# One unit of look-ahead between two halves of a matmul group, extended to the first block of a fused FFT + MoE kernel

## Chip, cores and metric

The kernel runs as one program on one core of a Trainium2 chip. Its metric is the device time of an execution in microseconds (us); the median of three runs stands for a kernel.

## The reference, cut to what matters

```python
X = np.fft.fft(x, axis=1)             # x: (8, 3072, 256)
X = np.fft.fft(X, axis=2).real        # -> tokens (24576, 256)
h = X @ w_in                          # first MoE layer, d_ff = 2048
g = h * (1.0 / (1.0 + np.exp(-1.702 * h)))
x2 = g @ w_out
logits = x2 @ w_gate                  # 8 experts, one expert for each token, with a capacity
# each kept token: gate * relu(x2 @ w1[e]) @ w2[e], all others stay 0
```

## The kernel before, in words

The FFT over the sequence is a matmul with cosine and sine tables on TensorE (tile `pf`, line 546). Its result goes to DRAM (`uv`). The FFT over the 256 columns is folded into the first layer's weights, which a *conversion* at the start turns into a table `G`, 2048 columns wide.

Then comes phase 2, which makes the routing logits of every token. For each of 8 batches there are 4 *blocks* of some 384 frequencies, and each block has 16 *units* (`f` from 0 to 15), one for each 128 hidden columns. A unit has two halves:

- **E** (`m1_even`, line 755): three matmuls into a PSUM bank `eo`. VectorE then makes a tile `e` from that bank (line 757).
- **O** (`m1_odd`, line 768): three more matmuls, accumulated into the *same* bank. VectorE then makes `h` (tile `h` or `g`, line 770) from `e` and the bank.

O adds to the bank that VectorE's `e` has to read first, so O of a unit can't begin before `e` of that unit is done. After O, ScalarE applies the gelu in place (lines 782 and 783, issued one unit later, in `gelu`), and every fourth unit TensorE multiplies the finished tiles into the block's logits (tile `acc`, line 792). There are 4 `eo` banks, which rotate.

I write E3 or O3 for the halves of unit 3 of the first block, and e3 for its tile `e`. All engines run their own instructions in the order in which the program is written; there is no scheduler. So the order of the lines in `phase2` is the order of each engine's queue.

In the first block of the first batch the conversion is still going on between the units. One weight slice follows another: VectorE and ScalarE convert a slice, TensorE transposes it (`psT`, line 274) or multiplies it by a DFT matrix (`psG`, line 250), ScalarE and VectorE copy the result into a piece of `G` (lines 253 and 254), and small matmuls `psc` (line 262) and `psW` (line 283) make a correction and a part of the router's weights. Batch 0's last FFT matmuls (`pf`) are spread over the units 0 to 4 as well. After unit 10 the conversion's memory is given back, and the loads of the next batch's input (`xc`, line 309) begin in it; line 397 is ScalarE's first use of them. In units 8 to 12 the second block's operand is prepared: transposes `psuv` (line 726), copied to `uvt` by ScalarE and VectorE (lines 731, 732), and a broadcast `psb` (line 741).

Of the kernel before, what the change touches and what calls it, by code (L numbers as in the profile page):

```python
# [23 lines left out]
B, S, D = 8, 3072, 256  # L24
# [10 lines left out]
NFC = DFF // P  # L35
# [8 lines left out]
NU, CONV, OWN, START1, START = 64, 10, 18, 26, 0  # L44
# [16 lines left out]
TICKS, WAIT0 = range(0, 13, 2), (2, 0, 1, 0, 1, 0, 1, 0)  # L61
AGE = (0, 2, 3, 4, 6)
HALVES = 1
HP, GP, LOGITS = 3, 6, 4


# [111 lines left out]
class K:  # L178
# [334 lines left out]
    def merge_half(self, b):  # L513


        x = self.half[b] = self.scp.tile([P, 4 * ZW], F16, tag="half", bufs=HALVES, name="half")
        for l, t in enumerate((self.hi[b, 1], self.lo[b, 1])):
# [508 lines left out]
    def phase2(self):  # L1026
        nc = self.nc
        self.lt, self.info, self.addr = {}, {}, {}
        self.hn = 0
        blocks = [(b, i) for b in range(B) for i in range(4)]  # L1030

        self.parts = [[([(0, 3, 0)], 0, 3)], [([(3, 3, 0)], 3, 3)], [([(6, 3, 0)], 6, 3)],
                      [([(9, 3, 0), (0, 4, 1), (4, 4, 1), (8, 4, 1)], 9, 15)]]
        self.whole = [([(0, 4), (4, 4), (8, 4)], 0, 24)]
        gs, pend, after = {}, [], []
        clears = self.clears()
        hprev, evens = None, []
        accs = {}

        def flush_logits():  # L1040
            j, q, tiles = pend.pop(0)
            b, i = blocks[j]
            if q == 0:
                accs[j] = self.bank("acc", "acc")
            self.m1_logits(b, i, q, tiles, accs[j])
            if q == NFC // 2 - 1:
                after.append((b, i, accs.pop(j)))

        def evac():
            while after:  # L1050
                b, i, acc = after.pop(0)
                self.m1_evac(b, i, acc)

        def gelu(hp):
            j, f, h = hp
            gs.setdefault((j, f // 2), []).append(self.m1_gelu(*blocks[j], f, *h))
            if f % 2 == 1:
                pend.append((j, f // 2, gs.pop((j, f // 2))))

        pre, post = self.timetable()  # L1060

        def take(todo):
            while todo:
                next(todo.pop(0), None)

        for j, (b, i) in enumerate(blocks):
            for f in range(NFC):
                if j == 0:
                    next(self.conv, None)
                evac()  # L1070
                take(pre[NFC * j + f])
                u = NFC * j + f
                while len(evens) < min(1 if u < NFC - 1 else 2, NU * B - u):
                    v = u + len(evens)
                    evens.append(self.m1_even(*blocks[v // NFC], v % NFC))
                self.now = evens[-1][1]
                if hprev is not None:
                    gelu(hprev)
                hprev = (j, f, self.m1_odd(b, i, f, *evens.pop(0)))
                if f % LOGITS == 1:  # L1080
                    while pend:
                        flush_logits()
                if j == 0:
                    next(self.conv, None)
                take(post[NFC * j + f])
                if f == 8 and j >= 4:
                    next(clears, None)
        gelu(hprev)
        while pend:
            flush_logits()  # L1090
        evac()
        self.last_route()
# [348 lines left out]
```

## Time and profile before

| | |
|---|---|
| three runs | 1908.97, 1911.43, 1918.87 us; median 1911.43 |
| profiled execution | 1909.04 us, of which the span from the first to the last instruction is 1907.3 us |
| mean granted TensorE clock | 0.981 of full speed |
| busy share of the span | TensorE 96%, VectorE 61%, ScalarE 50%, GpSimd 32% |

The busy shares are means over the whole execution, and it has stages with different limits; the stage that the change touches lies between 65 and 156 us. The granted clock is 1.0 at 2.4 GHz and 0.5 at 1.2 GHz. In a timeline a bracket gives the engine's idle time just ahead of a row and what ended it.

### The profile page before, as it was taken

To read this page: it belongs to the slowest core of one execution; us is meant where nothing else is said; L and a number is where in the kernel's file an instruction comes from. 1 tells how busy PE (TensorE), PEld (TensorE's weight loads), DVE (VectorE), ACT (ScalarE), POOL (GpSimd) and SP (SyncE) were. 2 spreads that over 40 slices of the span, in tenths; PEclk is the share of its full clock that TensorE was granted. 3 is DMA by queue.
4 is the path that set the end of the run, shared out by engine and by line. 5 is a ranking of instruction groups with operands and counts; after the bars stand their busy time and mean duration, and the time that the engine had idled before them with its cause. 6 is when DMAs were issued, how large, how long until landed. Compare 5 with 4: busy or idle time off the path is not lost.

```text
span 1907.3 us, 34052 instructions
## 1 busy us (share of the span) xinstructions
PE 1824.4 (96%) x12801; PEld 1600.1 (84%) x12801; DVE 1169.6 (61%) x2498; ACT 957.6 (50%) x2133; POOL 608.9 (32%) x776
## 2 busy tenths in 40 slices
PE   3879999999999999999999799999999999999998
PEld 3756778777778787877876599999999999999998
DVE  9636687686867768677689554444444454545442
ACT  5436776676766767766666233333333232333322
POOL 5006437539084481832318511111111100111101
PEclk9778999999999999999999899999999999999999
DMA  8411324232332323222112011111101010101000
GB/s 300 138 59 51 104 66 130 79 108 88 100 100 68 118 80 114 83 67 79 51 55 59 15 56 40 37 42 34 45 24 55 15 50 16 42 28 44 23 9 17
DMA packets 104181, 128.26 MB, mean 67 GB/s; under 512 B 15540, under 2 KB 89636, under 8 KB 103760
## 3 DMA queue, kind: packets, MB, share of 16 engines
q1 hardware_dynamic: 91992, 112.92, 18.6%
q0 software_dynamic: 11008, 12.82, 2.5%
q8 instruction: 100, 1.64, 0.4%
q14 instruction: 65, 0.53, 0.1%
q10 hardware_dynamic: 1016, 0.35, 0.1%
HBM read 77.54 MB, written 47.62 MB: 66 GB/s over the span
## 4 chain that ended last, share of the span: by engine, by line
PE 85%; DVE 8%; issue 4%; ACT 1%; POOL 1%; DMA 1%; POOLq 0%; ACTq 0%; DVEq 0%; SPq 0%
PE pkh L1200 14%; PE py L1214 14%; PE eo L768 13%; PE eo L755 12%; PE acc L792 9%; PE pod L1247 7%; PE pku L1233 7%; PE pf L546 6%; DVE e L757 3%; PE psG L250 1%; PE psuv L726 1%; DVE lo L489 1%; DVE g L770 1%; PE psL L830 1%; PE psb L741 1%
## 5 line engine op out<-in xcount | busy, mean ns | idle before, releaser
L757 DVE SCALAR_TENSOR_TENSOR e<-ub,cf,eo 128x384 f32<-128x384 f32 (+1 forms) x512 | 312.9, 611 | 204.0 <-PE eo L755 186.3
L768 PE MATMUL eo<-uvt,G 128*128 128x384 f32 (+1 forms) x1536 | 365.2, 346 | 31.9 <-DVE e L757 30.5
L755 PE MATMUL eo<-uvt,G 128*128 128x384 f32 (+1 forms) x1536 | 384.2, 358 | 0.3
L768 PEld LDWEIGHTS eo<-uvt,G 128*128 128x128 f32 x1536 | 272.5, 190 | 57.4 <-DVE e L757 56.3
L1200 PE MATMUL pkh<-kx,G 128*128 128x384 f32 x1536 | 310.5, 340 | 0.1
L1214 PE MATMUL py<-kg,wo 128*128 128x384 f32 x1536 | 307.1, 337 | 0.0
L755 PEld LDWEIGHTS eo<-uvt,G 128*128 128x128 f32 x1536 | 258.7, 190 | 40.2 <-issue 36.9
L1214 PEld LDWEIGHTS py<-kg,wo 128*128 128x128 f32 x1536 | 272.1, 187 | 0.0
L1257 POOL DMA_INDIRECT out_dram<-ko,tl x48 | 50.3, 1048 | 690.0 <-ACT ko L1256 680.2
L1200 PEld LDWEIGHTS pkh<-kx,G 128*128 128x128 f32 x1536 | 265.9, 189 | 0.8 <-ACT kx L1190 0.5
L1203 ACT ACTIVATE kgf<-pkh 128x384 f32<-128x384 f32 x256 | 125.8, 492 | 269.0 <-PE pkh L1200 180.7
L782 ACT ACTIVATE g<-g 128x384 f32<-128x384 f32 (+1 forms) x341 | 179.0, 525 | 145.0 <-DVE g L770 134.3
L1204 DVE CAST kg<-kgf 128x384 fp32r<-128x384 f32 x256 | 95.8, 374 | 218.5 <-ACT kgf L1203 217.6
L916 POOL DMA_INDIRECT table<-info,ad x192 | 190.3, 991 | 50.6 <-issue 47.6
L770 DVE SCALAR_TENSOR_TENSOR g<-e,eo 128x384 f32<-128x384 f32 (+1 forms) x341 | 187.3, 549 | 11.1 <-PE eo L768 11.1
L783 ACT ACTIVATE g<-eo 128x384 f32<-128x384 f32 (+1 forms) x341 | 163.8, 480 | 0.2
L1235 ACT ACTIVATE krl<-pku 128x384 fp32r<-128x384 f32 x128 | 62.9, 492 | 197.7 <-PE pku L1233 197.7
L1247 PE MATMUL pod<-w,krl 128*128 128x256 f32 x1152 | 156.6, 280 | 0.0
L792 PE MATMUL acc<-g,wog 128*32 128x384 f32 (+1 forms) x1364 | 156.2, 494 | 0.1
L1236 DVE SCALAR_TENSOR_TENSOR krl<-pku,krl 128x384 fp32r<-128x384 f32 x128 | 71.4, 558 | 138.5 <-ACT krl L1235 138.5
L1233 PE MATMUL pku<-ky,w 128*128 128x384 f32 x768 | 155.5, 338 | 0.6 <-ACT ky L1221 0.4
L1247 PEld LDWEIGHTS pod<-w,krl 128*128 128x128 f32 x1152 | 151.5, 188 | 0.0
(224 smaller groups left out, 2473.6 us busy)
## 6 DMA issues: line engine op xcount, KB each, us to landing
out_dram<-zero SPq DMA_DIRECT2D x24, 1024.0 KB
xc<-in_x_dram SPq DMA_DIRECT2D x42, 520.0 KB
stage<-in_w_dram SPq DMA_DIRECT2D x64, 256.0 KB
rt<-uvflat SPq DMA_DIRECT2D x32, 384.0 KB
f<-in_w_in_dram SPq DMA_DIRECT2D x7, 512.0 KB
f<-in_w_out_dram SPq DMA_DIRECT2D x7, 512.0 KB
x<-in_x_dram SPq DMA_DIRECT2D x6, 520.0 KB
uvflat<-ra SPq DMA_DIRECT2D x24, 128.0 KB
```

What stands on the lines that cost most here:

```text
L755: nc.tensor.matmul(ps[:, :n2], self.G[:, 0, a, fs], x[:, 0, c, :n2], start=(q == 0), stop=(q == 2))
L757: nc.vector.scalar_tensor_tensor(e[:, :n], self.ub[b, i][:, :n], self.cf[:, f:f + 1], ps[:, :n], op0=ALU.mult, op1=ALU.add)
L768: nc.tensor.matmul(ps[:, :n2], self.G[:, 1, a, fs], x[:, 1, c, :n2], start=False, stop=(q == 2), skip_group_check=True)
L770: nc.vector.scalar_tensor_tensor(h[:, 1, :n], e[:, :n], 2.0, ps[:, :n], op0=ALU.mult, op1=ALU.subtract)
L782: self.nc.scalar.activation(h[:, 1, :n], h[:, 1, :n], AF.Gelu_apprx_sigmoid)
L783: self.nc.scalar.activation(h[:, 0, :n], ps[:, :n], AF.Gelu_apprx_sigmoid)
L792: nc.tensor.matmul(acc[c:c + 32, :n], self.wog[:, 2 * q + j, :], gs[j][:, s, :n], start=(q == 0), stop=(q == NFC // 2 - 1))
L916: ins = nc.gpsimd.indirect_dma_start(out=self.table, out_offset=bass.IndirectOffsetOnAxis(ap=self.addr[b, t0][:, c:c + 1], axis=0), in_=se ...
L1200: nc.tensor.matmul(ps[:, :BS], self.G[:, h, a, fs], x[:, h, c], start=(q == 0), stop=(q == 5))
L1214: nc.tensor.matmul(self.py[n][k][:, :BS], self.wo[:, f, a, k * P:(k + 1) * P], g2[:, c], start=(f == 0 and a == 0 and c == 0), stop=(f == ...
L1233: nc.tensor.matmul(ps[:, :BS], w1[:, k, a, fs], y[:, k, c], start=(q == 0), stop=(q == 5))
L1247: nc.tensor.matmul(ps, r[:, c, t * P:(t + 1) * P], w2[:, F, a, :], start=(F == 0 and c == 0 and a == 0 and t != 1), stop=(F == F2 // P - 1 ...
```

## The change

The limit on how many E may be issued ahead was 1 in the units 0 to 14 of the whole program (no look-ahead: E of a unit right ahead of its own O) and 2 from unit 15 on (E of the next unit stands ahead of O). Now it is 2 from the first unit.

```diff
+AHEAD = 1
...
                 u = NFC * j + f
-                while len(evens) < min(1 if u < NFC - 1 else 2, NU * B - u):
+                while len(evens) < min(AHEAD + 1, NU * B - u):
                     v = u + len(evens)
                     evens.append(self.m1_even(*blocks[v // NFC], v % NFC))
```

`NFC` is 16, `NU` 64 and `B` 8. Lines below the added one have a number higher by one in the changed kernel. No instruction is added or taken away.

TensorE's queue at the start of the block, before (bank `eo_835` is unit 0's):

```order
L741 MATMUL psb_799<-uvt_707,selr_76 128x384 x2
L755 MATMUL eo_835<-uvt_707,G_285 128x384 x3
L768 MATMUL eo_835<-uvt_707,G_285 128x384 x3
L274 MATMUL psT_847<-c_ident_131,wa_644 128x128 x4
L546 LDWEIGHTS t_uee_137
```

and now (`eo_841` is unit 1's bank):

```order
L742 MATMUL psb_799<-uvt_707,selr_76 128x384 x2
L756 MATMUL eo_835<-uvt_707,G_285 128x384 x3
L756 MATMUL eo_841<-uvt_707,G_285 128x384 x3
L769 MATMUL eo_835<-uvt_707,G_285 128x384 x3
L275 MATMUL psT_853<-c_ident_131,wa_644 128x128 x4
L547 LDWEIGHTS t_uee_137
```

E1 has moved ahead of O0, and so on in each unit up to 15.

VectorE's queue at the same place, before (`wa`, `wq`, `wm`, `wl` are tiles of the conversion):

```order
L757 SCALAR_TENSOR_TENSOR e_839<-ub_802,cf_77,eo_835 128x384
L770 SCALAR_TENSOR_TENSOR h_844<-e_839,eo_835 128x384
L220 TENSOR_SCALAR wa_852<-f_746 128x512
L224 SCALAR_TENSOR_TENSOR wa_785<-wm_786,wa_785 128x512
L235 TENSOR_TENSOR wq_795<-wl_736,wq_795 128x512
L222 SCALAR_TENSOR_TENSOR wa_852<-f_746,wa_852 128x512
L227 TENSOR_SCALAR wq_861<-wa_785 128x512
L237 TENSOR_TENSOR wa_734<-wq_795,wa_734 128x512
L757 SCALAR_TENSOR_TENSOR e_890<-ub_802,cf_77,eo_886 128x384
L770 SCALAR_TENSOR_TENSOR h_897<-e_890,eo_886 128x384
```

and now:

```order
L758 SCALAR_TENSOR_TENSOR e_839<-ub_802,cf_77,eo_835 128x384
L758 SCALAR_TENSOR_TENSOR e_845<-ub_802,cf_77,eo_841 128x384
L771 SCALAR_TENSOR_TENSOR h_850<-e_839,eo_835 128x384
L221 TENSOR_SCALAR wa_858<-f_746 128x512
L225 SCALAR_TENSOR_TENSOR wa_785<-wm_786,wa_785 128x512
L236 TENSOR_TENSOR wq_795<-wl_736,wq_795 128x512
L223 SCALAR_TENSOR_TENSOR wa_858<-f_746,wa_858 128x512
L228 TENSOR_SCALAR wq_867<-wa_785 128x512
L238 TENSOR_TENSOR wa_734<-wq_795,wa_734 128x512
L758 SCALAR_TENSOR_TENSOR e_896<-ub_802,cf_77,eo_892 128x384
L771 SCALAR_TENSOR_TENSOR h_903<-e_845,eo_841 128x384
```

The six operations of the conversion now stand between e1 and O1's `h_903`; before, e1 (`e_890`) came behind them.

TensorE's queue at the end of the conversion, from unit 9's `psW` on, before (`eo_1268`, `eo_1308` and `eo_1325` are the banks of the units 10, 11 and 12):

```order
L283 MATMUL psW_1262<-wg_298,wt_1236 128x8 x4
L755 MATMUL eo_1268<-uvt_707,G_285 128x384 x3
L768 MATMUL eo_1268<-uvt_707,G_285 128x384 x3
L726 MATMUL psuv_1285<-c_ident_131,rt_1143 128x128 x3
L755 MATMUL eo_1308<-uvt_707,G_285 128x384 x3
L768 MATMUL eo_1308<-uvt_707,G_285 128x384 x3
L755 MATMUL eo_1325<-uvt_707,G_285 128x384 x3
L768 MATMUL eo_1325<-uvt_707,G_285 128x384 x3
L741 MATMUL psb_1338<-uvt_1226,selr_76 128x384 x2
```

and now (`eo_1246`, `eo_1274`, `eo_1314` and `eo_1331` are those of the units 10, 11, 12 and 13):

```order
L284 MATMUL psW_1268<-wg_298,wt_1242 128x8 x4
L756 MATMUL eo_1274<-uvt_707,G_285 128x384 x3
L769 MATMUL eo_1246<-uvt_707,G_285 128x384 x3
L727 MATMUL psuv_1291<-c_ident_131,rt_1149 128x128 x3
L756 MATMUL eo_1314<-uvt_707,G_285 128x384 x3
L769 MATMUL eo_1274<-uvt_707,G_285 128x384 x3
L756 MATMUL eo_1331<-uvt_707,G_285 128x384 x3
L769 MATMUL eo_1314<-uvt_707,G_285 128x384 x3
L742 MATMUL psb_1344<-uvt_1232,selr_76 128x384 x2
```

Between `psW` and O12 there are now E11, O10, `psuv`, E12, O11 and E13. On VectorE the second copy into `uvt` (line 732), which needs that `psuv`, stood ahead of e11 before and stands ahead of e12 now.

## Rows read from the trace of the kernel before

**Rows 1.** The page's busy times, and the granted clock in 40 equal slices.

```profile
PE 1824.4 (96%) x12801; PEld 1600.1 (84%) x12801; DVE 1169.6 (61%) x2498; ACT 957.6 (50%) x2133; POOL 608.9 (32%) x776
PEclk9778999999999999999999899999999999999999
```

**Rows 2.** TensorE's waits from 65 to 157 us: in total, times, longest.

```profile
PE eo L768 <- DVE e L757: 20.5, 16, 3.8
```

**Rows 3.** TensorE's waits from 157 to 1040 us, the other 31 blocks.

```profile
PE eo L768 <- DVE e L757: 8.4, 23, 1.2
```

**Rows 4.** TensorE's timeline, first block: start, duration, group, idle ahead of it.

```profile
69.78 1.33 PE L768 MATMUL eo<-uvt,G 128*128 128x384 f32 x3 [3.75 <-DVE e L757]
...
74.50 1.31 PE L755 MATMUL eo<-uvt,G 128*128 128x384 f32 x3
76.52 1.33 PE L768 MATMUL eo<-uvt,G 128*128 128x384 f32 x3 [0.71 <-DVE e L757]
...
92.19 1.33 PE L768 MATMUL eo<-uvt,G 128*128 128x384 f32 x3 [1.78 <-DVE e L757]
...
102.11 1.09 PE L768 MATMUL eo<-uvt,G 128*128 128x384 f32 x3 [1.82 <-DVE e L757]
...
118.93 0.79 PE L768 MATMUL eo<-uvt,G 128*128 128x384 f32 x3 [1.41 <-DVE e L757]
...
141.42 1.33 PE L768 MATMUL eo<-uvt,G 128*128 128x384 f32 x3 [3.49 <-DVE e L757]
```

**Rows 5.** Stretches of the first block: busy time by engine, TensorE's clock, DMA.

```profile
68.25:85.25 17.00, 14.76 (x67) 12.95 (x68) 8.76 (x19) 4.80 (x10) 0.20 (x1) 0.50 0.19 58
85.25:92.00 6.75, 4.20 (x36) 3.52 (x34) 5.23 (x10) 5.42 (x14) 0.00 (x0) 0.99 0.45 155
92.00:99.00 7.00, 6.81 (x22) 5.78 (x23) 3.17 (x7) 0.00 (x0) 0.00 (x0) 0.51 0.00 0
99.00:102.25 3.25, 1.43 (x14) 1.07 (x13) 1.21 (x2) 2.45 (x7) 0.00 (x0) 1.00 0.32 84
102.25:116.00 13.75, 13.02 (x52) 9.33 (x53) 6.25 (x12) 2.33 (x7) 0.00 (x0) 0.51 0.15 48
116.00:139.75 23.75, 16.99 (x114) 13.20 (x112) 8.87 (x15) 8.26 (x21) 0.98 (x1) 1.00 0.19 63
139.75:153.50 13.75, 10.52 (x36) 6.44 (x36) 4.08 (x8) 5.43 (x14) 10.77 (x16) 0.51 0.32 107
```

The columns of rows 5 are the stretch, its length, then busy us (and instructions) of PE, PEld, DVE, ACT and POOL, the granted clock, the share of the DMA engines and GB/s.

**Rows 6.** VectorE's timeline ahead of O0.

```profile
67.60 0.69 DVE L254 TENSOR_TENSOR G<-psG,G 128x512 fp32r<-128x512 f32 x1 [2.87 <-ACT G L253]
...
69.12 0.61 DVE L757 SCALAR_TENSOR_TENSOR e<-ub,cf,eo 128x384 f32<-128x384 f32 x1
```

**Rows 7.** The chain that ended last, around the end of the conversion.

```profile
133.97 1.00 PE psW L283 x8
135.03 3.58 DMA xc<-in_x_dram
138.71 1.16 ACT f L397 x2
141.42 1.33 PE eo L768 x3
```

**Rows 8.** TensorE's timeline in the second block (at full clock), and at `psuv`.

```profile
136.91 0.49 PE L726 MATMUL psuv<-c_ident,rt 128*128 128x128 f32 x3
...
156.72 0.70 PE L755 MATMUL eo<-uvt,G 128*128 128x384 f32 x3
157.25 0.70 PE L768 MATMUL eo<-uvt,G 128*128 128x384 f32 x3
```

**Rows 9.** Groups from 0 to 300 us: the conversion's matmuls `psG`.

```profile
L250 PE MATMUL psG<-wa,c_dft 128*128 128x256 f32 x64 | 23.9, 538 | 0.0
```

**Rows 10.** End of GpSimd's folds of batch 1, and ScalarE's first use of the last.

```profile
183.49 0.47 POOL L416 TENSOR_TENSOR f<-ev 128x128 f32<-128x128 f32 x1
...
200.17 0.71 ACT L487 ACTIVATE hi<-f,sc 128x516 f16<-128x516 f32 x1
```

## The prediction

> **What bounds the kernel now.** I read the page first. TensorE is busy 96% of the span, and its granted clock is down in slices 2 to 4, some 48 to 190 us, and hardly anywhere else [rows 1]. The first block lies there, so that is the place to look, and what counts there is when TensorE moves on.
>
> The second view is TensorE's waits. In the first block all of them are of one kind: O waits for the tile `e` of its own unit, 16 times in 16 units, 20.5 us in total [rows 2]. In the 31 blocks behind it, which already issue one E ahead, the same kind of wait comes 23 times in 496 units and costs 8.4 us [rows 3]: 0.02 us a unit against 1.28. The conversion's own matmuls, `psG` for one, are not waited for: 0.0 us of idle ahead of them [rows 9].
>
> The third view is the timeline [rows 4]. The wait is a bare round trip in about half of the units (0.71 us: end of E, `e` on VectorE, start of O). It is longer where `e` stands behind something else in VectorE's queue: 1.41 to 1.82 us behind a copy into `G`, 3.75 us at O0, 3.49 us at O11.
>
> The fourth view cuts the block by clock [rows 5]. Four stretches run at 0.50 or 0.51, that is 1.2 GHz. TensorE is busy 14.76, 6.81, 13.02 and 10.52 us in them, 45.1 us. The clock falls just after a wait of 3.75, 1.78, 1.82 and 3.49 us [rows 4, 5]; after the 1.41 us at 118.93 it stays up. So the waits cost twice: as idle time, and as half speed behind them.
>
> **The change, part by part.** The sum is made against the profiled execution, 1909.0 us, which is 2.4 us below the median of the three runs.
>
> *Waits removed: -20.5 us.* E of the next unit now stands ahead of O, so `e` of O's own unit was asked for a whole unit earlier. Between E and its O lie the O of the unit before, the conversion's matmuls and one more E, against a round trip of 0.7 us and at worst 1.8. That this is cover enough is what the other 31 blocks show [rows 3].
>
> *Waits that stay: +6.5 us.* O0 has no unit ahead of it. Its `e` starts at 69.12 because VectorE first waits for ScalarE's copy of `G` and then does three evictions [rows 6]; E1 does not alter that, it only fills 0.53 us of the wait (the pitch from E to O at full clock, 156.72 to 157.25 [rows 8]). 3.75 - 0.53 = 3.2 us stay. The second is the 3.49 us at O11. There ScalarE's queue stands at its first use of `xc`, whose load starts when `psW` ends; the copies into `uvt` stand behind it, and `e` behind these [rows 7]. From the end of `psW` to O11 it takes 141.42 - 134.97 = 6.45 us. The same chain now ends at O12, since `e` of unit 11 has moved ahead of the copy. In front of O12 TensorE has five halves and `psuv`: 5 x 0.53 + 0.49 = 3.1 us [rows 8]. So 3.3 us stay, late by one unit. Both could shrink to nothing only if the load or the copies came earlier, so the bound below is 0.
>
> *Clock: -22.6 us, if it stays up.* 45.1 us of TensorE's work at half clock take half as long at full clock [rows 5]. The bounds are 0 (clock as now) and 22.6.
>
> *VectorE as the next bound: +1.7 us.* From 68.25 to 116.00 VectorE is busy 8.76 + 5.23 + 3.17 + 1.21 + 6.25 = 24.6 us. TensorE's work there, with the half-clock stretches halved, is 7.4 + 4.2 + 3.4 + 1.4 + 6.5 = 22.9 us [rows 5]. So in the units 0 to 5, while slices are converted, VectorE is the longer one by 1.7 us, and TensorE must wait that much somewhere. Behind 116 us it has 8.87 + 4.08 against 17.0 + 5.3 and is no bound.
>
> *Falls of the clock that stay: +5.0 us.* The two waits that stay are longer than those of 1.78 and 1.82 us that brought the clock down [rows 4, 5], so it may fall behind each. At worst the first and the last half-clock stretch stay as they are and keep 14.76 / 2 + 10.52 / 2 = 12.7 us; at best nothing. The work behind O12 has no more waits in it, and E1 now fills a part of the first. I take two fifths of the bound, 5.0 us: about one fall, at the start.
>
> [...] In the trace TensorE works without a wait from 69.78 to the end of E1 at 75.81, and the clock is still at 0.50 until 85.25 [rows 4, 5]. [...]
>
> *What costs nothing.* No instruction and no byte is added. A bank of `eo` is taken one unit earlier, with the 4 banks and the look-ahead that all later blocks have; there nothing but 8.4 us of waits for `e` shows [rows 3]. On VectorE `h` of a unit now stands behind `e` of the next, 0.6 us [rows 6]; the gelu that needs it is issued a unit later, the logits matmul up to four. What is late next: the load of `xc` follows `psW` [rows 7] and moves forward with it, by nearly all of the gain ahead of 135 us. GpSimd's folds, which start with that load, move by as much, while TensorE gains some 8 us more behind it (10.52 / 2 and four waits of 0.71). The last fold ends at 183.49 + 0.47 and is first used at 200.17 [rows 10], 16 us of slack, which covers that. Behind the first block nothing hangs on a fixed time, so the gain should reach the end.
>
> *Sum:* 1909.0 - 20.5 + 6.5 - 22.6 + 1.7 + 5.0 = 1879.1 us.
>
> **The rivals.**
>
> *The waits go, the clock does not come back.* The conversion's narrow matmuls (`psW`, `psc`) stay between the units, and half clock held on through unbroken work [rows 4, 5]. Against it: at 116 to 139.75 the clock was full with TensorE busy only 17.0 of 23.75 us [rows 5], less than it will be after the change. Time: 1909.0 - 20.5 + 6.5 + 1.7 = 1897.
>
> *VectorE's waits for the copy of `G` stay as long as they are.* VectorE idles ahead of that copy (2.87 us in [rows 6]), and `e` of the next unit and `h` of this one stand behind it. If it could not convert in that time, the stretch up to 116 us would not get shorter, and only what lies behind would: waits of 1.41 twice and 0.71 five times, 0.18, and 5.3 us of clock, about 12 us. Against it: TensorE does not wait for the conversion now [rows 9], and the copy waits for `psG`, which itself takes half the time at full clock. Time: 1897.
>
> *No change.* A fixed time would have to hold the block's end, the landing of `xc` being the only candidate. It would let TensorE run ahead to O12 instead of O11, 2 or 3 us, and keep the rest: 1906. Against it, the load's start is `psW`'s end [rows 7].
>
> *Slower.* TensorE does its matmuls in the order of the queue, so if E of the next unit has to wait for its bank, the O behind it waits too, which it did not before. The bank comes free with the gelu three units back, on ScalarE, whose queue can stand at a load as it does at `xc`. Each such stop would cost up to 3.3 us, as there. To be 0.5% slower than now, all 16 units would have to lose 2.8 us each (1918.6 less 1874.1, by 16), and ScalarE is busy only 4.8 of 17.0 us in the first stretch [rows 5]. Time if it held in every unit: 16 x 3.3 = 53 us on 1874, 1927.
>
> **How the numbers follow.** About 0.5%, 9.5 us, is what a measurement of this kernel can tell from no change. The forecast has a chance of 0.73, with a range of its own from 1867 to 1889. The clock that stays down has 0.14, `G`'s copy 0.05, no change 0.06, slower 0.02. The first three are faster by over 0.5%: 0.92. The range reaches down to where neither wait nor half clock is left, 1909.0 - 20.5 - 22.6 = 1866, and up to 1897, where two rivals lie. The predicted time is 1879.
>
> **What would show it.** In the first block O's waits for `e` should shrink from 16 to a few, two of them over 3 us, at O0 and at O12. O12 should follow `psW` by about 6.5 us. The second block should begin some 30 us earlier, at 123 to 127 us instead of 155, and everything behind should keep that distance. The granted clock should be 1.0 in most of the block, with a half-clock stretch behind O0 at most some 14 us long. It is wrong if `psT`, `psG` or `psc` show waits of more than 2 or 3 us together (VectorE or ScalarE would then set the pace), if E shows waits for ScalarE, if half clock still covers over 25 us of the block, or if what is gained by 130 us is lost again further on, where a fall of the clock could come at another place than now.

## The result, and the profile after

The changed kernel takes 1883.01 us (median of four runs, 1879.51 to 1893.14) beside 1911.71 us for the kernel before in the same comparison: a ratio of 0.9853, 95% interval 0.9813 to 0.9892, or 28 us less. The prediction was 1879, with a range from 1866 to 1897 and 0.92 for faster. It held.

First the page of the changed kernel, which answers to [rows 1].

```profile
PE 1815.1 (96%) x12801; PEld 1594.4 (84%) x12801; DVE 1167.9 (62%) x2498; ACT 956.2 (51%) x2133; POOL 607.8 (32%) x776
PEclk9799999999999999999999899999999999999999
```

The dip of the clock in the slices 2 to 4 has shrunk. The second view is TensorE's waits from 65 to 129 us, the first block of the changed kernel, beside [rows 2]:

```profile
PE eo L769 <- DVE e L758: 6.6, 2, 3.3
PE psc L263 <- DVE G L255: 0.2, 1, 0.2
```

Sixteen waits have become two. TensorE's timeline shows where they are (beside [rows 4]):

```profile
68.59 1.21 PE L756 MATMUL eo<-uvt,G 128*128 128x384 f32 x6
73.05 0.79 PE L769 MATMUL eo<-uvt,G 128*128 128x384 f32 x3 [3.24 <-DVE e L758]
...
101.72 0.78 PE L756 MATMUL eo<-uvt,G 128*128 128x384 f32 x3
102.33 0.69 PE L769 MATMUL eo<-uvt,G 128*128 128x384 f32 x3
102.86 0.60 PE L275 MATMUL psT<-c_ident,wa 128*128 128x128 f32 x4
...
113.60 1.06 PE L284 MATMUL psW<-wg,wt 128*128 128x8 f32 x8
...
121.08 0.78 PE L769 MATMUL eo<-uvt,G 128*128 128x384 f32 x3 [3.35 <-DVE e L758]
...
127.34 0.68 PE L756 MATMUL eo<-uvt,G 128*128 128x384 f32 x3
```

The first row is E0 and E1 in one piece, the second O0. Then come E and O of the units 7 and 6 with the `psT` behind them, `psW` of unit 9, and O12. O12 starts 121.08 - 114.66 = 6.4 us after the end of `psW`. The last row is E of the second block's first unit; from E0 to it the block took 127.34 - 68.59 = 58.75 us, and 89.9 us before.

The fourth view cuts the block by clock, with the columns of [rows 5]. The first row here is the whole block of the kernel before, all the others are of the changed kernel:

```profile
65.25:155.25 90.00, 69.70 (x345) 53.93 (x344) 39.08 (x73) 30.54 (x71) 11.95 (x17) 0.72 0.22 74
```

```profile
68.50:74.50 6.00, 2.76 (x22) 2.39 (x21) 3.27 (x8) 2.39 (x6) 0.20 (x1) 0.99 0.45 152
74.50:84.75 10.25, 10.25 (x42) 9.10 (x41) 6.66 (x13) 3.84 (x7) 0.00 (x0) 0.51 0.15 53
84.75:122.25 37.50, 33.91 (x260) 29.77 (x258) 26.15 (x50) 20.74 (x52) 3.66 (x4) 1.00 0.31 103
122.25:125.75 3.50, 3.50 (x18) 1.87 (x20) 1.40 (x3) 3.29 (x8) 3.34 (x5) 0.52 0.45 154
...
68.50:127.50 59.00, 52.16 (x345) 44.45 (x344) 37.96 (x73) 30.26 (x71) 8.95 (x11) 0.88 0.31 103
```

The reader is to see three things. TensorE ran the same 345 matmuls in both blocks, in 69.70 us of busy time before and in 52.16 us now. Its idle time was 90.00 - 69.70 = 20.3 us and is 59.00 - 52.16 = 6.84 us, which is the two lines of waits above. And the clock falls twice, each time 1 to 1.5 us after the end of a wait that stayed: 10.25 and 3.50 us at half clock.

The chain that ended last, at O12, beside [rows 7]:

```profile
113.67 1.00 PE psW L284 x8
114.67 0.02 SPq L310
114.69 0.03 issue
114.72 3.54 DMA xc<-in_x_dram
...
118.37 1.16 ACT f L398 x2
119.53 0.39 ACT uvt L732
...
120.42 0.62 DVE e L758
121.03 0.04 issue
121.08 0.78 PE eo L769 x3
```

It is the chain of before, one unit later in the program and 20 us earlier in time: the load of `xc` starts when `psW` ends.

**One execution is not the kernel.** The profiled execution is the slowest of the four, 1893.14 us, and its distance to that of before shrinks behind the block. I use the row that makes `ub` (one for each block, on ScalarE) as a milestone. The table gives its first, third and last start, and the two distances, for the profiled execution of each kernel (e1 to e12 are the experiments below).

| kernel | first | third | last | first to third | third to last | whole |
|---|---|---|---|---|---|---|
| before | 65.54 | 177.13 | 1024.28 | 111.6 | 847.2 | 1909.04 |
| changed | 68.79 | 148.86 | 1003.47 | 80.1 | 854.6 | 1893.14 |
| e1, changed again | 64.42 | 147.23 | 994.53 | 82.8 | 847.3 | 1879.03 |
| e10, changed again | 64.39 | 144.76 | 999.29 | 80.4 | 854.5 | 1886.87 |
| e12, before with constants moved | 69.46 | 173.79 | 1028.43 | 104.3 | 854.6 | 1914.41 |

From the first to the third row the three executions of the changed kernel are 28.8 to 31.5 us shorter than the profiled execution of before. The 29 blocks behind that take 847 or 854.6 us, and this does not go with the change: e12 does not have it and takes 854.6 us, e1 has it and takes 847.3. The experiments ran in three jobs, each on another chip. All four kernels of the last job (e9 to e12) took 854.5 to 854.7 us, all eight of the two jobs before it 847.1 to 847.3; whether this belongs to the job or to the chip is open. Behind the third row the profiled execution lost 12.4 us of its lead (28.3 to 15.9 us): 7.5 of them are this pitch, and 4.9 come behind the last row. Ahead of the block it had lost 3.25 us, in work that the change does not touch: two stretches at half clock, from 43.75 to 50.5 and from 60.75 to 67.75, lasted about twice as long as those of before (44.25 to 47.75 and 61.5 to 65).

### The profile page after: what moved, and what is told of

It reads as the page before. It is cut to its first block, busy times and chain, and to the rows that moved or that the text cites. A ratio compares the mean times of both kernels' runs of the same rounds, so it can differ in the third digit from the quotient of the medians.

```text
span 1891.4 us, 34055 instructions
## 1 busy us (share of the span) xinstructions
PE 1815.1 (96%) x12801; PEld 1594.4 (84%) x12801; DVE 1167.9 (62%) x2498; ACT 956.2 (51%) x2133; POOL 607.8 (32%) x776
## 4 chain that ended last, share of the span: by engine, by line
PE 85%; DVE 9%; issue 4%; ACT 1%; DMA 1%; POOL 0%; ACTq 0%; POOLq 0%; DVEq 0%; SPq 0%
PE pkh L1201 14%; PE py L1215 14%; PE eo L769 13%; PE eo L756 12%; PE acc L793 9%; PE pod L1248 7%; PE pku L1234 7%; PE pf L547 6%; DVE e L758 3%; PE psG L251 1%; PE psuv L727 1%; DVE lo L490 1%; DVE g L771 1%; PE psL L831 1%; PE psb L742 1%
## 5 line engine op out<-in xcount | busy, mean ns | idle before, releaser
L769 PE MATMUL eo<-uvt,G 128*128 128x384 f32 (+1 forms) x1536 | 361.9, 344 | 21.9 <-DVE e L758 20.3
```

The costliest lines, as they stand in the source:

```text
L769: nc.tensor.matmul(ps[:, :n2], self.G[:, 1, a, fs], x[:, 1, c, :n2], start=False, stop=(q == 2), skip_group_check=True)
```

## The experiments

**e1: the changed kernel again, unaltered.** 

> The changed kernel once more, unaltered. Its profiled execution of 1893.1 us lay some 10 us above its other runs, and had lost in phases 2 and 3 part of the 31 us that the first block gained. If that is a matter of one execution, this one's trace keeps 28 to 32 us to the end and the time is 1880 to 1885. If the look-ahead costs something in every batch (the other theory), the distance to the kernel before shrinks again from 28 us at the second block to some 20 us at the end of phase 2.

 Measured: 1879.63 us beside 1907.38, ratio 0.9853 (0.9818 to 0.9887). Its waits in the block are again two for `e`, at O0 (3.31 us) and at O12 (3.69 us). The clock falls behind the first, and within the second, which ends at 118.72:

```profile
69.25:83.00 13.75, 13.75 (x69) 12.44 (x67) 7.28 (x14) 4.61 (x10) 0.20 (x1) 0.51 0.21 70
117.00:123.75 6.75, 5.03 (x19) 3.78 (x23) 3.79 (x7) 4.98 (x14) 6.44 (x8) 0.50 0.37 134
```

So the gain repeats, and the length of a fall does not: 13.75 us behind O0 here, 10.25 us in the first execution, though TensorE was busy all through both.

**e2 and e3: one half of the block each.** The look-ahead in units 0 to 7 alone (e2), and from unit 8 on (e3).

```diff
-                while len(evens) < min(AHEAD + 1, NU * B - u):
+                while len(evens) < min(2 if u < 8 or u >= NFC - 1 else 1, NU * B - u):   # e2
+                while len(evens) < min(2 if u >= 8 else 1, NU * B - u):                  # e3
```

> Look-ahead in the units 0 to 7 of the first block alone. My theory (a wait costs its idle time and the half clock behind it): waits of 11.9 us less 3.2 that stay at O0, clock 34.6 / 2 = 17.3 less 5.0, VectorE 1.7 back: 19.3 us faster, 1892. If the waits alone count: 7 us faster, 1905. The units 8 to 14 should show the old waits, 3.5 us at O11 among them.

 

> Look-ahead from unit 8 on alone. My theory: waits of 8.6 us less 3.3 that stay at O12, clock 10.5 / 2 = 5.3 less up to 2.5: 8 to 10.6 us faster, 1901 to 1904. If the waits alone count: 5 us faster, 1906. With the run of the units 0 to 7 it should add up to the whole gain of 28.7 us if each wait's price is local.

 Measured: e2 1881.92 us, ratio 0.987 (0.9841 to 0.9899), 25 us less than before; e3 1896.4 us, 0.9951 (0.9928 to 0.9973), 9 us less. The waits are in the units expected, 10.5 us (8 times) in e2 and 18.2 us (10 times) in e3; by the expectations they add up to 8.6 + 3.2 = 11.8 and 11.9 + 3.3 = 15.2. e3's time is as expected; e2 gained 25 us where 19 were expected. The sum of the halves, 34 us, is more than the whole, 28, so the price of a wait is not local. In e2 the clock did not fall behind O0, after a wait of 3.23 us:

```profile
70.27 0.79 PE L769 MATMUL eo<-uvt,G 128*128 128x384 f32 x3 [3.23 <-DVE e L758]
```

and the only half clock in its block lies from 112.75 to 126.5 us. So the falls of the clock do not add up from the halves; why this fall did not come I can't say.

**e4: the clock alone.** The kernel before, with matmuls of 128 columns put into the waits, into the bank that the next E takes; nothing reads their result. The O do not start earlier by them; only TensorE is less idle.

```diff
+FILL = (50, 8, 10, 24, 24, 8, 18, 8, 18, 8, 8, 44, 8, 8, 8)
...
-        ps = self.peo.tile([P, 512], F32, tag="eo", bufs=EO, name="eo")
+        bank = lambda: self.peo.tile([P, 512], F32, tag="eo", bufs=EO, name="eo")
+        ps = self.spare.pop() if self.spare else bank()
...
+        if b == 0 and i == 0 and f < len(FILL):
+            self.spare.append(bank())
+            for _ in range(FILL[f]):
+                nc.tensor.matmul(self.spare[0][:, :P], self.tbl["uee"][:, 0, 0, :P], self.hi[0, 0][:, :P], start=True, stop=True)
```

> The kernel before, without look-ahead, with wide matmuls into an unused bank between E and O of the first block, as many as fit into each wait at full clock less some 0.25 us. They compute nothing that is read. O still waits for its e, so no wait is shortened; only TensorE's idle time is filled. My theory (the clock falls because of the idle time in the waits): the block runs at full clock, 45.1 / 2 = 22.6 us less what the first fall keeps, 17 to 22 us faster than before, 1890 to 1895. The rival (the conversion's narrow matmuls hold the clock down, waits or not): the half-clock stretches stay, and the time is 1912 or some us more.

 Measured: 1897.34 us, ratio 0.9949 (0.9932 to 0.9966), 10 us less than before; from the first to the third `ub` 12.6 us less than the profiled execution of before. The windows by clock:

```profile
67.00:77.25 10.25, 7.67 (x95) 6.96 (x92) 6.28 (x13) 5.99 (x12) 0.30 (x1) 1.00 0.45 134
77.25:84.00 6.75, 6.75 (x22) 5.72 (x23) 3.03 (x6) 0.24 (x1) 0.00 (x0) 0.50 0.20 68
84.00:104.50 20.50, 16.97 (x172) 15.10 (x170) 13.78 (x26) 10.38 (x25) 0.00 (x0) 1.00 0.30 88
104.50:108.00 3.50, 3.50 (x21) 1.12 (x20) 2.10 (x4) 0.00 (x0) 0.00 (x0) 0.52 0.19 58
108.00:148.00 40.00, 36.44 (x313) 29.85 (x313) 16.78 (x30) 15.68 (x39) 11.77 (x16) 1.00 0.23 75
```

Half clock covers 10.25 us of the block, and 51.5 in the profiled execution of before. It is not that execution alone: the mean clock was 0.989 to 0.991 in all eight runs of e4 and 0.980 to 0.987 in the thirteen of before in this job. So TensorE's waits have a part in bringing the clock down, and the conversion's narrow matmuls, which are all still there, do not hold it down. That it is the idle time, and not the lack of the work that I added, e4 alone does not tell; the changed kernel speaks for it, where 260 of the same matmuls ran at 1.00 for 37.50 us with none added. The clock is worth something by itself: 10 to 13 us. That is less than the 17 to 22 that I expected; where the other 5 us went I did not settle. In this kernel O still waits for the conversion on VectorE and for `xc`, which do not go by TensorE's clock.

**e5: the folds of batch 1 later.** The folds are the first work on the next batch's input `xc`. `fold_steps` yields three times more after its first loads, so ScalarE's first use of `xc` stands behind its copies into `uvt`.

```diff
+HOLD = 3
...
+        for _ in range(hold):
+            yield
         for n, _ in enumerate(self.fft_folds(b)):
...
-        spread(self.fold_steps(1), FSTEPS, CONV, START1 + 4)
+        spread(self.fold_steps(1, HOLD), FSTEPS + HOLD, CONV, START1 + 4)
```

> The changed kernel with the folds of batch 1 put some two units later; their loads of xc stay where they are, so ScalarE's first use of xc stands behind its copies into uvt. Theory (O12 waits because the copies into uvt stand behind that first use, and the clock falls behind O12 because TensorE was idle there): the wait of 3.3 to 3.7 us at O12 goes, no half-clock stretch follows it (3.5 and 6.75 us of it in the two executions seen), and the time falls by about 5 us against the changed kernel, 1875 where that takes 1880 (ratio to before 0.983). Rival (O12 waits for something else that is late, such as the matmuls psuv or their copies): the wait stays over 2 us, and the time is that of the changed kernel. Second rival (the folds are now late themselves): a wait of about the same size at a later O, or ahead of the second batch.

 Measured: 1876.55 us, ratio 0.9847 (0.9817 to 0.9876): 1 us by the ratios, which is within their intervals, and not 5. The wait at O12 is gone, as the theory had it. Of the waits from 40 to 160 us the two longest kinds are now

```profile
PE eo L770 <- DVE e L759: 3.3, 1, 3.3
PE psuv L728 <- DMA rt<-uvflat: 2.5, 1, 2.5
```

and the clock falls within that second wait, from 136.5 to 140. This is the second rival, in a form that I had not named: `rt`, a later block's operand on its way back from `uv`, comes late by SyncE's queue (e7 shows it).

**e6: the constants off ScalarE's queue.** In the changed kernel ScalarE issues three loads between `ub` and the copy into `G` that VectorE, and through it `e0`, waits for:

```profile
68.79 0.49 ACT L745 ACTIVATE ub<-psb 128x384 f32<-128x384 f32 x1 [5.41 <-PE psb L742]
68.80 0.35 ACTq L196 DMA_DIRECT2D c_iota<-in_c_iota_dram  x1
69.19 0.45 ACTq L196 DMA_DIRECT2D c_tri<-in_c_tri_dram  x1
69.68 0.44 ACTq L196 DMA_DIRECT2D c_token<-in_c_token_dram  x1
70.17 0.18 ACT L286 ACTIVATE wog<-psW 128x16 f32<-128x16 f32 x1 [0.88 <-issue]
70.25 0.59 ACT L254 ACTIVATE G<-psG 128x512 fp32r<-128x512 f32 x1
```

```diff
-        self.iota8 = self.load(lp, "c_iota")
+        self.iota8 = self.load(lp, "c_iota", eng=nc.sync)   # and c_tri, c_token alike
```

> The changed kernel with the three loads of constants that stand on ScalarE's queue between ub and the copy into G issued on SyncE's queue instead. Theory (O0 waits because VectorE's three evictions ahead of e0 wait for that copy, which ScalarE begins only after issuing the three loads, from 68.80 to 70.12 in the changed kernel): the wait at O0 shrinks from 3.3 to 2.0 to 2.5 us and the time by about 1 us, 1879 where the changed kernel takes 1880, which is less than can be told apart in the time but not in the trace. Rival (the copy waits for psG): the wait at O0 stays at 3.2 to 3.4 us. The half-clock stretch behind O0 stays by either.

 Measured: 1872.34 us, ratio 0.9826 (0.9798 to 0.9854). That is 5 us, where 1 was expected. The wait shrank as the theory said:

```profile
69.20 0.79 PE L769 MATMUL eo<-uvt,G 128*128 128x384 f32 x3 [2.26 <-DVE e L758]
```

and the clock stayed up behind it, which I had not expected:

```profile
66.00:112.00 46.00, 40.48 (x309) 35.65 (x307) 34.98 (x69) 25.97 (x62) 2.29 (x3) 1.00 0.40 128
112.00:115.50 3.50, 3.02 (x10) 3.03 (x11) 2.02 (x5) 2.68 (x7) 3.34 (x5) 0.52 0.32 97
```

**e7: e5 and e6 together.** 

> The changed kernel with the folds of batch 1 later and the three loads of constants on SyncE's queue. If both parts act where I say, one wait of 2.0 to 2.5 us for e is left in the first block (at O0), against 6.6 to 7.0 us in the changed kernel, and one half-clock stretch at most. Time about 6 us under the changed kernel, 1874 where that takes 1880 (ratio to before 0.982). If the wait at O0 is now short enough for the clock to stay up, another 5 to 7 us less. If the waits only move to other places, no change.

 Measured: 1873.24 us, ratio 0.983 (0.9805 to 0.9856). No half clock is left in the block, but the wait of 2.4 us for `rt` has the place of that at O12, and the time is e6's. On SyncE's queue (SPq) one sees why:

```profile
107.12 0.83 SPq L311 DMA_DIRECT2D xc<-in_x_dram  x2
...
109.03 19.02 SPq L311 DMA_DIRECT2D xc<-in_x_dram  x4
128.11 0.96 SPq L711 DMA_DIRECT2D rt<-uvflat  x2
```

The later loads of `xc` need buffers that the folds give back, so they hold the queue for 19.02 us: in this stretch SyncE waits 10.1 us for GpSimd's `pe` and 7.5 us for ScalarE's `f`, both of the folds. The load of `rt` stands behind them.

**e8: e7 with the wait at O0 filled,** by 32 matmuls as in e4. 

> The kernel before this one, with 32 more matmuls of 128 columns put between E1 and O0, into the bank that E2 takes next; nothing reads their result, and the output is the reference's. They fill the wait at O0 with some 2 us of work. Theory (the clock falls behind O0 because TensorE stands idle there): no half-clock stretch behind O0, where the changed kernel has 10.25 to 13.75 us of one, and the time falls by another 5 to 7 us, 1868 where the changed kernel takes 1880 (ratio to before 0.979). Rival (the clock falls for another reason, such as the conversion's narrow matmuls behind O0 or work at the end of the phase before): the half-clock stretch stays within 10 to 14 us and the time is that of the kernel before this one.

 Measured: 1871.87 us, ratio 0.9827 (0.9804 to 0.9851). O0's wait is 0.44 us, and nothing is gained on e7: the clock had not fallen there any more. The expectation missed, since e6's edit had already taken away the fall that e8 was to remove.

**e9: e7 with the load of `rt` for the third block ahead of the loads of `xc`.**

```diff
     def m1_prep(self, b, i):
-        self.m1_load(b, i)
+        if (b, i) != (0, 2):
+            self.m1_load(b, i)
...
     def fold_steps(self, b, hold=0):
+        if hold:
+            self.m1_load(0, 2)
```

> Both parts together (folds later, constants on SyncE's queue), and the load rt of the third block issued ahead of the loads of xc. In the kernel without this last edit TensorE waited 2.4 us at psuv for rt, whose load stood on SyncE's queue behind the fourth load of xc, which held the queue for 19 us. Theory: that wait goes, and with it some 2.4 us; ratio to before 0.9815 where the kernel without it had 0.983; from the first to the third ub row about 70 us instead of 72.7. Rival: something else is as late (the copies into uvt, the folds), and the 72.7 us stay.

 Measured: 1876.24 us beside 1912.58, ratio 0.981 (0.9794 to 0.9826), and 70.1 us from the first to the third `ub`. Its waits from 65 to 140 us:

```profile
PE eo L770 <- DVE e L759: 2.2, 1, 2.2
PE eo L757 <- ACT h L785: 0.5, 1, 0.5
PE psc L264 <- DVE G L256: 0.2, 1, 0.2
```

The wait for `rt` is gone. This is the version with the lowest ratio, though its interval overlaps those of e6, e7 and e8. In its own job it is 10.6 us under the unaltered changed kernel, with no run of the one (1874.82 to 1879.37) within those of the other (1882.36 to 1887.98).

**e10 and e11: the changed kernel and e6 once more, side by side.** 

> The changed kernel once more, unaltered, beside the next kernel. Two of its executions showed 10.25 and 13.75 us at half clock behind O0. I expect the same here, about 82 us from the first to the third ub row, and a ratio to before of 0.985.

 

> The changed kernel with the three loads of constants on SyncE's queue once more. It gained 5 us on the changed kernel where 1 was expected, because no half-clock stretch followed a wait of 2.26 us at O0. If that was the edit: again no half clock behind O0, 74 us from the first to the third ub row, and a ratio to before of 0.982 to 0.983, some 5 us under the unaltered changed kernel of this job. If it was that execution: half clock of 10 us or more behind O0, 80 us or more, and 1 us under it.

 Measured: e10 1886.87 us, ratio 0.9857 (0.984 to 0.9875); e11 1881.13 us, 0.9833 (0.9817 to 0.9848). In e10 the clock falls behind O0 once more, in e11 it does not (wait of 2.25 us). The first to the third `ub` take 80.4 and 74.2 us. The medians lie 5.7 us apart, and the runs overlap only at their ends (1882.36 and 1882.45 us). So e6's 5 us were the edit and not that execution.

**e12: the kernel before, with e6's edit.** 

> The kernel before with the three loads of constants on SyncE's queue, without the look-ahead. The wait at O0 shrinks from 3.75 us to some 2.7. If the wait at O0 alone decides whether the clock falls behind it, the half-clock stretch of 17 us at the start of the block goes and the time falls by up to 8 us (1900 where before takes 1908). If the waits of 0.7 to 1.8 us in the units behind it bring the clock down as well, a half-clock stretch of over 10 us begins a few units later instead, and 1 to 3 us are gained.

 Measured: 1912.71 us, ratio 0.9995 (0.9984 to 1.0007): nothing, less than either theory gave. The wait at O0 is 2.77 us and the clock stays up behind it, but it falls behind the wait of 1.77 us at O1 instead, and three times more. The second theory had this fall, with a longer stretch and a gain of 1 to 3 us. Four of the 16 waits:

```profile
72.72 0.79 PE L768 MATMUL eo<-uvt,G 128*128 128x384 f32 x3 [2.77 <-DVE e L757]
77.76 0.79 PE L768 MATMUL eo<-uvt,G 128*128 128x384 f32 x3 [1.77 <-DVE e L757]
...
107.46 0.79 PE L768 MATMUL eo<-uvt,G 128*128 128x384 f32 x3 [2.39 <-DVE e L757]
...
138.90 0.79 PE L768 MATMUL eo<-uvt,G 128*128 128x384 f32 x3 [3.36 <-DVE e L757]
```

Half clock covers 78.5 to 85.5, 92.25 to 99, 119.5 to 123 and 140 to 150.25 us. So the edit paid 5 us where the look-ahead had already taken the other waits, and nothing here.

## Why the prediction was right

Its terms against the rows of the block:

| term | predicted, us | measured, us |
|---|---|---|
| waits for `e`, removed and staying | -20.5 + 6.5 = -14.0 | 20.3 to 6.6: -13.7 |
| VectorE as the next bound | +1.7 | +0.2 (`psc`) |
| clock, with the falls that stay | -22.6 + 5.0 = -17.6 | busy 69.70 to 52.16: -17.5, of which clock -22.55 + 6.9 = -15.65 |
| the block | -29.9 | -31.0 |

- **What bounds the kernel.** Right: the block became 31 us shorter in the profiled executions, and the whole kernel 28 us by the ratio of all runs.
- **The waits that stay.** Right in number, place and size: O0 with 3.24 us, O12 with 3.35 us, 6.4 us behind `psW`. e5 shows the reason for O12, since that wait went with its cause. At O0 the copy of `G` was late in part by the three loads that ScalarE issues ahead of it, which the prediction did not see; e6 shows that they are 1.0 us of the 3.24.
- **VectorE.** Mis-sized: TensorE waits 0.2 us for it in the block. In the changed kernel the clock is at half in the units where VectorE was to be the longer one, and VectorE is busy 6.66 of the 10.25 us there. e6 has the same units at full clock:

```profile
68.25:93.00 24.75, 23.56 (x191) 21.07 (x191) 23.85 (x48) 14.34 (x33) 0.20 (x1) 1.00 0.45 137
```

VectorE is busy 23.85 us and TensorE 23.56, of 24.75: level, not 1.7 us apart as I had it from halved busy times (24.6 against 22.9). I expect that VectorE would set the pace here if TensorE became faster still; no run shows it.
- **The clock.** The sum was right and one size in it was not. I took two fifths of the bound of 12.7 us (14.76 / 2 + 10.52 / 2 is 12.64), about one fall. There were two in each of three executions, and TensorE's busy time in them was 13.75, 18.78 and 13.5 us, half of which is lost: 6.9, 9.4 and 6.75 us. That the sum holds nevertheless is luck: TensorE's busy time at full clock came out 1.9 us shorter than that of before (52.16 - 6.9 against 69.70 - 22.55), a term that the prediction did not have. Two rows of the kernel before, around O6 (118.93 in [rows 4]), suggest where it comes from:

```profile
116.75 0.77 PE L755 MATMUL eo<-uvt,G 128*128 128x384 f32 x3
...
119.56 0.60 PE L274 MATMUL psT<-c_ident,wa 128*128 128x128 f32 x4
```

With a wait behind it E counts as busy for 0.77 us, and `psT` starts 0.63 us after O6. In the changed kernel the next half starts 0.61 us after E (101.72 to 102.33), and `psT` 0.53 us after O6. That is some 0.26 us a unit at full clock, and 14 units lost their wait, so by this estimate (3.6 us at most) it is more than enough for the 1.9.
- **When the clock falls.** The prediction has it fall just after four waits. By its own rows it fell in the middle of two of them: at 68.25, where the wait at O0 ran to 69.78, and at 139.75, where that at O11 ran to 141.42. The sum counts only busy time at half clock and is not touched by this.
- **How long a fall lasts.** Behind O0 TensorE was busy 10.25 of 10.25 us, and in e1 13.75 of 13.75 us, with the clock at 0.51; the fall behind O12 lasted 3.50 us. The prediction had read from the rows of before that the clock can stay at half through unbroken work, and at O0 it did.
- **The rivals.** The clock came back: 37.50 us at 1.00 with 64 of the narrow matmuls `psc` and `psW` among the 260. `G`'s copy did not keep the stretch of the units 0 to 5 as long as it was: from O0 to O6 it is 102.33 - 73.05 = 29.3 us, where it was 118.93 - 69.78 = 49.15. (In the price of that rival one wait of 0.71 us is missing: behind 116 us there were six and not five.) The load of `xc` started at 114.72, when `psW` ended, so nothing fixed the block's end. No E waited for ScalarE in the block; behind it one did, for 0.4 us.
- **That the gain reaches the end.** It did, by the `ub` rows of e1: 29.9 us at the third, of which 1.1 lie ahead of the block, and 29.75 us at the last. The single execution of the first comparison would have said otherwise.

What stays open is how much of the 28 us is the clock. e4 gives 10 to 13 us to it alone; by the busy time of the two profiled blocks it is 17.5. The kernel before itself ran from 1899.99 us (mean clock 0.988) to 1910.52 us (0.981) in one job, so its profiled execution, at 0.981, stands at the slow end. The sum began from that execution, so its clock term fits it better than the kernel in general: e12, with all 16 waits (22.4 us), had 27.5 us at half clock in its block where that one had 51.5, and by the median was not faster.

## What to carry to other kernels

A wait of TensorE is to be counted with the work behind it: here 13.7 us less of idle time came with 17.5 us less of busy time in the profiled executions, some 15.6 of them the clock. When most such waits are gone, each one that is left is worth tracing to its cause by the chain, as a load issue on ScalarE's queue (5 us, where the wait shrank by 1) or a queue held by a load that waits for its buffer (`rt`). The edit of the load issues was worth nothing in the kernel that still had the other waits, so small edits are to be tried again after a large one.

## What was unexpected of the hardware

The length of a wait does not tell whether the clock falls. It fell at waits of 1.31 us (e4, at 77.25) and 1.77 us (e12, at 78.5), and stayed up behind 2.39 and 2.77 us (e12), 3.23 us (e2) and 2.25 or 2.26 us (e6, e7, e9 and e11, each time). At O0 of the changed kernel it fell in all three executions. Nor does a fall need a long wait: in ten of the fourteen profiled executions, that of before and the first of the changed kernel among them, one began between 59.75 and 63.5 us, ahead of the block, where no wait in the 9 us before it was longer than 0.66 us. In e1, e3, e6 and e9 the clock stayed up there, with the same waits. So the waits are one cause of the falls and not the only one; what else decides is open. And the pitch of the blocks behind was 0.9% longer in one job than in two others, for each of their kernels: 854.6 against 847.2 us.
